# Both first experts freeze 384 slots in the last chunk of moe1, and expert 1's first layer is written ahead of expert 0's last slots

## The chip, the core and the metric

The kernel runs on one core of a Trainium2 chip. The metric is the device time of one execution in microseconds (us). Engines are named as the profile names them: PE is TensorE, ACT ScalarE, DVE VectorE, POOL GpSimd, and SP the engine that only issues transfers here.

## The reference, cut to what matters

Three stages follow each other: block-causal attention on 4 x 8 heads of 576 x 64, a dense gated layer on the 2304 tokens ("moe1"), and a mixture of eight experts with two experts for each token.

```
x   = attention(q, k, v)                  # 2304 x 512
x   = ((x @ w1) * (x @ w2)) @ w3 @ w_out  # moe1, inner width 1024
n   = x @ w_gate + log1p(exp(x @ w_noise)) * noise
top2, top2_w = the two largest of n, softmax over the two
for e in range(8):                        # the experts
    h = relu(x[tokens of e] @ m1[e])      # 512 -> 1024, "first layer"
    out[tokens of e] += top2_w * (h @ m2[e])   # 1024 -> 512, "second layer"
```

## The kernel before

Every product is made of three matmuls of float32r high and low parts (`mm3`, L470 to L472, on PE). What splits a matrix into the two parts is `split` (L457): a cast on ACT for the high part (L461) and a subtraction on DVE, or on POOL, for the low part (L465).

moe1 walks over nine chunks of 256 tokens. In a chunk, `ab` (L194) makes the gated product in eight steps f, and `yout` (L210) multiplies it with the folded product of w3 and w_out, which lies in the four weight buffers `pc[8]` to `pc[11]`. The router of a chunk (L249) runs one chunk later, in small pieces between these steps. At its end it scatters token numbers into a table in DRAM, `idt`, with four indirect transfers of 128 rows from POOL (L337), and SP writes the chunk's rows of y to DRAM, to `yt` (L356).

Each expert has 640 slots in the table, as five tiles of 128 ("slot tiles" 0 to 4). Slot tiles 0 to 2 are part s = 0, slot tiles 3 and 4 part s = 1. The work of an expert e on a part is: `gather` (L875), one indirect transfer from POOL for each slot tile, which reads 128 rows of y; `trans` (L884), four PE transposes a tile and a split into `xt`; `ffn1` (L896), the first layer, eight steps f of 12 matmuls, ended by a relu on ACT (L905) and a low part on DVE (L906); and `ffn2` (L908), the second layer, 24 matmuls a slot tile, ended by a scaling on ACT into the tile `yo` (L919) and an indirect transfer from POOL that adds the rows to the output (L920). `yo` has two buffers, and `xt` and `ht` of each part have one.

`freeze` (L419), called in the last chunk after all eight steps f, takes the router's count after eight chunks and makes sure that slots 0 to 383 of expert 0 are not written by the last chunk; it then calls `start_early` (L858), in which SP loads the table's rows of these slots (L864, tile `ids0`) and POOL gathers them (tile `xga`, three buffers). So expert 0's part 0 (`trans`, `ffn1`, `ffn2` at L503 to L506) runs while the last router ends. Everything else is in `phase3` (L922): SP loads the whole table (L926, tile `ids`) behind the last scatters, loads weights, and POOL gathers the other slots.

Weights of the experts come as 64 pieces of 0.5 MB, numbered n, eight for an expert (0 to 3 the first layer, 4 to 7 the second). `load_next` (L836) has SP load piece n into a staging tile and splits it into buffer `pc[ORDER[n % 12]]`. The first eight pieces are loaded early, in the last chunk, through the two staging tiles `xab` and `xr` (one buffer each); the others go through `stf` (three buffers) in `phase3`. Pieces 8 to 11, expert 1's first layer, go into `pc[8]` to `pc[11]`, which moe1 reads until its last `yout`.

A planner puts the instructions of each engine into one order from priorities and a model of durations, so the order on an engine isn't that of the code. Each engine then works strictly in its order.

Of the kernel before, what the change touches and what calls it, by code (L numbers as in the profile page):

```python
# [8 lines left out]
F32 = mybir.dt.float32  # L9
F32R = mybir.dt.float32r  # L10
BF16 = mybir.dt.bfloat16
I32 = mybir.dt.int32
I64 = mybir.dt.int64
AF = mybir.ActivationFunctionType
OP = mybir.AluOpType
# [7 lines left out]
P = 128  # L23
CAP = 640
NSLOT = CAP // P
NA = 3
# [55 lines left out]
class Moe1:  # L82
# [280 lines left out]
    def steps(self):  # L363

        state, due = {}, {}
        clock = [0]

        def ahead(c, last=3):

            step = state.get(c, 0)
            if c == NCH or step > last or clock[0] < due.get(c, 0) or (step == 0 and self.batches(c) > self.ready):
                return
            if step == 0:
                self.x_load(c)
            else:
                with ExitStack() as es:
                    for m in self.marks:
                        es.enter_context(self.tc.issue_after(m.ins))  # L380
                    self.x_prep(c, step - 1)
            state[c] = step + 1
            due[c] = clock[0] + (0 if c == 0 else AHEAD[step])

        for c in range(NCH):
            while state.get(c, 0) < 4:
                ahead(c)
                clock[0] += 2
                yield 0
            for f in range(8):  # L390
                while self.conv < 28 + 4 * (f // 2):
                    yield 0
                with self.tc.high_priority(offset=MOE_PRIO):
                    self.ab(c, f)
                self.tick(self.ticks)
                if c == NCH - 1 and f % 2 == 1:
                    self.k.load_next()
                    self.k.load_next()
                ahead(c + 1, 2)
                clock[0] += 1  # L400
                yield 2.67
            ahead(c + 1)
            if c == NCH - 1:
                for _ in self.rt:
                    pass
                self.freeze()
            for t in range(TPC):
                for part in range(2):
                    with self.tc.high_priority(offset=MOE_PRIO):
                        self.yout(c, t, part)  # L410
                    self.tick(self.ticks)
                    ahead(c + 1)
                    clock[0] += 1
                    yield 2.6
            for _ in self.rt:
                pass
            self.rt = self.router(c)

    def freeze(self):  # L419

        nc, p2, v = self.nc, self.p2, self.nc.vector
        cb = p2.tile([P, E], BF16, name="cb")
        v.tensor_copy(cb, self.run_cnt)
        pc = self.psR.tile([P, 512], F32, name="m")
        nc.tensor.matmul(pc[:, 0:1], self.tri[:, 1, :], cb[:, 0:1], start=True, stop=True)
        m = p2.tile([P, 1], F32, name="miss")
        v.tensor_tensor(m, self.room, pc[:, 0:1], op=OP.subtract)
        v.tensor_scalar(m, m, 0.0, float(NA), op0=OP.max, op1=OP.min)
        v.tensor_tensor(self.run_cnt[:, 0:1], self.run_cnt[:, 0:1], m, op=OP.add)
        self.k.start_early()  # L430

    def tail(self):
        nc, k, p2 = self.nc, self.k, self.p2
        self.ticks = 4
        self.psR = k.psT
        for _ in self.rest:
            pass
        for _ in self.rt:
            pass
        cb = p2.tile([P, E], BF16, name="cb")  # L440
        nc.vector.tensor_copy(cb, self.run_cnt)
        pcn = self.psR.tile([P, 512], F32, name="m")[:, 0:E]
        nc.tensor.matmul(pcn, self.tri[:, 1, :], cb, start=True, stop=True)
        cf = p2.tile([P, E + 1], F32, name="cf")
        nc.vector.tensor_copy(cf[:, 0:E], pcn)
        nc.vector.tensor_reduce(cf[:, E:], cf[:, 0:E], axis=AX, op=OP.max)
        nc.vector.tensor_copy(k.mxc, cf[:, E:])
        nc.vector.tensor_copy(k.cnt, cf[:, 0:E])


class Kernel:
# [23 lines left out]
    def run(self):  # L475
        tc, nc, a = self.tc, self.nc, self.a
        nc.scalar.preload_act_table_set("natural_log_exp_and_others")
        with ExitStack() as es:
            cp = es.enter_context(tc.tile_pool(name="cp", bufs=1))
            dr = es.enter_context(tc.tile_pool(name="dr", bufs=1, space=DRAM))  # L480
            self.cp = cp

            def dram(name, shape, dt=F32):
                return dr.tile(shape, dt, name=name)

            self.x2 = dram("x2", [BH, P, S])
            self.rs = dram("rs", [B, H, S])
            self.yt = dram("yt", [NT + P, ROW])
            self.idt = dram("idt", [E * TABR, 1], I32)
            self.ident = cp.tile([P, P], F32, name="ident")  # L490
            nc.sync.dma_start(self.ident, a["cst"][:, 0:128])
            self.pc = [cp.tile([P, 2, 1024], F32R, name=f"pc{i}") for i in range(12)]
            with ExitStack() as es2:
                self.psM = es2.enter_context(tc.tile_pool(name="psM", bufs=2, space=PSUM))
                with tc.tile_pool(name="p2", bufs=1) as self.p2:
                    self.moe1 = Moe1(self, self.p2, self.psM)
                    self.attention()
                    self.psT = es2.enter_context(tc.tile_pool(name="psT", bufs=2, space=PSUM, reuse_waits="tile"))
                    self.psH = es2.enter_context(tc.tile_pool(name="psH", bufs=4, space=PSUM, reuse_waits="tile"))
                    self.pa = es2.enter_context(tc.tile_pool(name="pa", bufs=1, side="right", reuse_waits="tile"))  # L500
                    self.early = True
                    self.moe1.tail()
                    self.trans(0, 0)  # L503
                    self.ffn1(0, 0)
                    for i in range(NA):
                        self.ffn2(0, i)  # L506
                    self.moe1.p2s.close()
                self.early = False
                self.phase3()
            self.overflow()  # L510
# [347 lines left out]
    def start_early(self):  # L858
        nc = self.nc
        self.xg, self.xt, self.ht, self.wv = {}, {}, {}, {}  # L860
        self.tab = self.idt.rearrange("(e s) o -> e (s o)", e=E)
        self.ids = self.pa.tile([P, E, NSLOT], I32, name="ids3")
        self.ids0 = self.pa.tile([P, NA], I32, name="ids0")
        nc.sync.dma_start(self.ids0, self.slots(self.tab, self.ids)[0][0][:, 0, :])  # L864
        self.gather(0, 0)

    def idx(self, e, i):
        ids = self.ids0[:, i:i + 1] if e == 0 and i < NA else self.ids[:, e, i:i + 1]
        return bass.IndirectOffsetOnAxis(ap=ids, axis=0)

    @staticmethod
# [3 lines left out]
    def gather(self, e, s):  # L875
        for i in self.part(s):
            if self.early:
                t = self.pa.tile([P, ROW], F32, name="xga", bufs=NA)
            else:
                t = self.pb.tile([P, ROW], F32, name="xg", bufs=8)  # L880
            self.xg[e, i] = t
            self.nc.gpsimd.indirect_dma_start(out=t, out_offset=None, in_=self.yt, in_offset=self.idx(e, i))
# [39 lines left out]
    def phase3(self):  # L922
        nc = self.nc
        with self.tc.tile_pool(name="pb", bufs=1, reuse_waits="tile") as self.pb:
            for src, dst in self.slots(self.tab, self.ids):
                nc.sync.dma_start(dst, src)  # L926
            for _ in range(4):
                self.load_next()
            self.gather(0, 1)
            self.gather(1, 0)  # L930
            self.gather(1, 1)
            for e in range(E):
                if e == 0:
                    self.trans(0, 1)
                else:
                    self.ffn1(e, 0)
                self.ffn1(e, 1)
                if e + 1 < E:
                    for s in range(2):
                        self.trans(e + 1, s)  # L940
                        if e + 2 < E:
                            self.gather(e + 2, s)
                for _ in range(4):
                    self.load_next()
                for i in range(0 if e else NA, NSLOT):
                    self.ffn2(e, i)
                for _ in range(4):
                    self.load_next()
# [96 lines left out]
```

## Time and profile before

| what | us |
|---|---|
| median of three runs | 1124.17 (1123.17 to 1125.45) |
| the profiled execution's own time | 1124.48 |
| its span, first to last instruction | 1122.7 |
| PE busy | 1056.7 (94%) |
| DVE, ACT, POOL busy | 575.1, 496.8, 367.5 |

All times in the text are counted from the start of the span of this one execution. moe1 ends at about 635 us, expert 0's part 0 at about 676 us, and the experts fill the rest. In the views of the trace a row names the line of the code, the engine, the operation and the tiles (output <- inputs). A bracket at a row's end tells how long the engine had stood idle before it and what ended that. The granted clock of TensorE is given as a share of full speed.

### The profile page before, as it was taken

Reading aid. Unit: us, or ns where it says so; the run is one execution under the profiler, and the core shown is the slowest. Engines: PE = TensorE matmul, PEld = TensorE weight load, DVE = VectorE, ACT = ScalarE, POOL = GpSimd, SP = SyncE. Lnnn points to the kernel's source line nnn. Section 1 sums busy time; section 2 is a strip of 40 time slices with the busy share of each in tenths; the row PEclk is TensorE's granted clock in tenths of the full one; section 3 lists DMA queues with packets and bytes.
Section 4 is the critical chain, followed back from the end, with each engine's and each line's share of the span. In section 5 each row is a group of like instructions: output and inputs, shape, how many; then the busy total and the mean of one; then the engine's idle time right before and its main releaser. Section 6 shows DMA issues by size and latency. Waiting matters only on the chain.

```text
span 1122.7 us, 17570 instructions
## 1 busy us (share of the span) xinstructions
PE 1056.7 (94%) x6588; PEld 945.3 (84%) x6588; DVE 575.1 (51%) x1229; ACT 496.8 (44%) x1180; POOL 367.5 (33%) x355
## 2 busy tenths in 40 slices
PE   5799978799999999999999898999999999999996
PEld 4577777698898989898999787989898989989894
DVE  6997779857475757653444434433334243424120
ACT  5765547565565647542234324433333333433120
POOL 4442445425243332523441326231312223120202
PEclk9998989998999999999999999999999999999998
DMA  9755775334615482524414227654444545351303
GB/s 231 247 185 164 197 174 193 95 93 119 165 63 117 142 207 76 116 70 81 77 38 95 86 81 224 187 141 104 133 112 123 122 123 122 104 113 30 38 10 40
DMA packets 79442, 135.81 MB, mean 121 GB/s; under 512 B 21005, under 2 KB 45813, under 8 KB 79349
## 3 DMA queue, kind: packets, MB, share of 16 engines
q1 hardware_dynamic: 69237, 113.44, 36.1%
q0 software_dynamic: 10112, 21.16, 10.2%
q8 instruction: 54, 0.88, 0.3%
q14 instruction: 39, 0.32, 0.1%
HBM read 103.92 MB, written 30.66 MB: 120 GB/s over the span
## 4 chain that ended last, share of the span: by engine, by line
PE 72%; DMA 10%; DVE 9%; issue 3%; ACT 2%; POOL 2%; SPq 2%; POOLq 0%; DVEq 0%; ACTq 0%
PE ph L470 12%; PE ph L472 12%; PE ph L471 12%; PE m L470 7%; PE m L471 7%; PE m L472 7%; PE tp L653 3%; PE av L678 3%; DMA stg<-in_w_dram 3%; DMA v<-in_v_dram 2%; PE sb L623 2%; PE sb L620 2%; DMA out_dram<-yo,ids 2%; DVE stf L529 2%; PE m L893 1%
## 5 line engine op out<-in xcount | busy, mean ns | idle before, releaser
L470 PE MATMUL m<-xh,pc 128*128 128x256 f32 x576 | 165.7, 291 | 2.0 <-DVE pc L465 0.8
L471 PE MATMUL m<-xh,pc 128*128 128x256 f32 x576 | 162.8, 287 | 3.1 <-DVE xh L465 3.1
L472 PE MATMUL m<-xh,pc 128*128 128x256 f32 x576 | 161.5, 287 | 0.3 <-POOL pc L465 0.3
L470 PE MATMUL ph<-xt,pc 128*128 128x256 f32 (+1 forms) x512 | 157.2, 309 | 4.8 <-issue 3.8
L471 PE MATMUL ph<-xt,pc 128*128 128x256 f32 (+1 forms) x512 | 157.8, 308 | 0.0
L472 PE MATMUL ph<-xt,pc 128*128 128x256 f32 (+1 forms) x512 | 157.5, 308 | 0.0
L920 POOL DMA_INDIRECT out_dram<-yo,ids x40 | 65.4, 1635 | 198.0 <-ACT yo L919 110.7
L906 DVE SCALAR_TENSOR_TENSOR ht<-ph,ht 128x256 fp32r<-128x256 f32 (+1 forms) x128 | 61.7, 489 | 130.3 <-ACT ht L905 129.7
L470 PE MATMUL ph<-pc,ht 128*128 128x512 f32 x320 | 128.0, 401 | 0.0
L471 PE MATMUL ph<-pc,ht 128*128 128x512 f32 x320 | 126.3, 395 | 0.0
L472 PE MATMUL ph<-pc,ht 128*128 128x512 f32 x320 | 126.2, 395 | 0.0
L461 ACT CAST pc<-stf 128x1024 fp32r<-128x1024 f32 (+1 forms) x96 | 82.1, 872 | 89.4 <-DMA stf<-in_m_dram 51.1
L465 DVE TENSOR_TENSOR pc<-stf,pc 128x1024 fp32r<-128x1024 f32 x56 | 67.4, 1226 | 104.7 <-ACT pc L461 97.6
L639 ACT ACTIVATE pb<-sb,nm 128x288 f32<-128x288 f32 (+3 forms) x192 | 93.6, 497 | 56.7 <-DVE nm L637 25.2
L470 PEld LDWEIGHTS m<-xh,pc 128*128 128x128 f32 x576 | 110.4, 193 | 4.2 <-DVE at L206 1.3
L471 PEld LDWEIGHTS m<-xh,pc 128*128 128x128 f32 x576 | 110.1, 193 | 4.3 <-DVE xh L465 3.7
L905 ACT ACTIVATE ht<-ph 128x256 fp32r<-128x256 f32 (+1 forms) x128 | 55.0, 437 | 127.6 <-PE ph L472 127.6
L472 PEld LDWEIGHTS m<-xh,pc 128*128 128x128 f32 x576 | 109.3, 193 | 1.2 <-POOL pc L465 0.8
L465 POOL TENSOR_TENSOR gt<-at,gt 128x256 fp32r<-128x256 f32 x72 | 57.8, 807 | 156.3 <-ACT gt L461 153.5
L653 PE MATMUL tp<-ident,pb 128*128 128x128 f32 x480 | 83.0, 289 | 23.3 <-ACT pb L639 8.4
L470 PEld LDWEIGHTS ph<-xt,pc 128*128 128x128 f32 x512 | 96.5, 189 | 5.6 <-issue 4.0
L634 DVE TENSOR_REDUCE nm<-sb 128x1 f32<-128x128 f32 (+2 forms) x192 | 79.2, 438 | 38.2 <-PE sb L623 32.9
(157 smaller groups left out, 2314.1 us busy)
## 6 DMA issues: line engine op xcount, KB each, us to landing
stf<-in_m_dram SPq DMA_DIRECT2D x56, 512.0 KB
qk<-in_qk_dram SPq DMA_DIRECT2D x32, 576.0 KB
stg<-in_w_dram SPq DMA_DIRECT2D x32, 512.0 KB
x<-ev SPq DMA_DIRECT2D x32, 288.0 KB
xab<-x SPq DMA_DIRECT2D x20, 256.0 KB
yt<-y SPq DMA_DIRECT2D x18, 260.0 KB
stg<-in_w_out_dram SPq DMA_DIRECT2D x8, 512.0 KB
v<-in_v_dram SPq DMA_DIRECT2D x24, 160.0 KB
```

The source lines that it names most:

```text
L461: d = nc.scalar.copy(h, src)
L465: return d, eng.tensor_tensor(l, src, r32(h), op=OP.subtract)
L470: nc.tensor.matmul(out, a, c, start=first, stop=False)
L471: nc.tensor.matmul(out, a, d, start=False, stop=False)
L472: nc.tensor.matmul(out, b, c, start=False, stop=last)
L634: nc.vector.tensor_reduce(nm[:, n:n + 1], o[:, 0:w], axis=AX, op=OP.max, negate=True)
L639: nc.scalar.activation(pb[t][:, k0:k0 + src.free_size()], src, AF.Exp, bias=nm, scale=1.0, accum_out=sums[:, h // H, t + n, h % H:h % H + 1])
L653: nc.tensor.transpose(bank[:, n * P:(n + 1) * P], pb[t][:, kt * P:(kt + 1) * P], self.ident)
L678: nc.tensor.matmul(c.av[:, o0:o0 + w], c.vv[:, kt, :], c.pt[:, i, s0:s0 + w], start=(kt == 0 and i == 0), stop=(kt == 4 and i == m - 1))
L905: nc.scalar.activation(hh[:, 0, f, :], ph, AF.Relu)
L906: nc.vector.scalar_tensor_tensor(hh[:, 1, f, :], ph, 0.0, r32(hh[:, 0, f, :]), op0=OP.max, op1=OP.subtract)
L920: nc.gpsimd.indirect_dma_start(out=self.a["out"], out_offset=self.idx(e, i), in_=yo, in_offset=None, compute_op=OP.add)
```

## The change

- `freeze` is called in the last chunk at step f = 5 and not after f = 7, and it freezes the 384 slots of expert 0 and of expert 1. `start_early` loads the table rows of both and gathers both (tile `xga` now has five buffers).
- The four pieces 8 to 11 are loaded in `tail`, through `xab` and `xr`, and no longer in `phase3` through `stf`.
- The whole table is loaded by POOL in two plain transfers (part 1's columns first), no longer by SP.
- Expert 0's part 1 is gathered early as well, and expert 1's `trans` and `ffn1` on part 0 are written ahead of `phase3`, that is, ahead of `trans` and `ffn1` of expert 0's part 1. `phase3` leaves out what has been done.

```diff
                 if c == NCH - 1 and f % 2 == 1:
                     self.k.load_next()
                     self.k.load_next()
+                if c == NCH - 1 and f == 5:
+                    for _ in self.rt:
+                        pass
+                    self.freeze()
...
             ahead(c + 1)
-            if c == NCH - 1:
-                for _ in self.rt:
-                    pass
-                self.freeze()
...
         for _ in self.rest:
             pass
+        for _ in range(4):
+            k.load_next()
         for _ in self.rt:
             pass
...
                     self.moe1.tail()
+                    for src, dst in reversed(self.slots(self.tab, self.ids)):
+                        nc.gpsimd.dma_start(dst, src)
+                    self.gather(0, 1)
                     self.trans(0, 0)
                     self.ffn1(0, 0)
                     for i in range(NA):
                         self.ffn2(0, i)
+                    self.trans(1, 0)
+                    self.ffn1(1, 0)
...
-        nc.sync.dma_start(self.ids0, self.slots(self.tab, self.ids)[0][0][:, 0, :])
+        nc.sync.dma_start(self.ids0, self.slots(self.tab, self.ids)[0][0][:, 0:2, :])
         self.gather(0, 0)
+        self.gather(1, 0)
...
-                t = self.pa.tile([P, ROW], F32, name="xga", bufs=NA)
+                t = self.pa.tile([P, ROW], F32, name="xga", bufs=NSLOT)
...
-            for src, dst in self.slots(self.tab, self.ids):
-                nc.sync.dma_start(dst, src)
-            for _ in range(4):
-                self.load_next()
-            self.gather(0, 1)
-            self.gather(1, 0)
             self.gather(1, 1)
             for e in range(E):
                 if e == 0:
                     self.trans(0, 1)
-                else:
+                elif e > 1:
                     self.ffn1(e, 0)
                 self.ffn1(e, 1)
                 if e + 1 < E:
                     for s in range(2):
-                        self.trans(e + 1, s)
+                        if e or s:
+                            self.trans(e + 1, s)
```

How the planner orders it is shown at three places. In these rows `pc_67` to `pc_78` are `pc[0]` to `pc[11]`, so `pc_75` to `pc_78` take the pieces 8 to 11; lines of the changed kernel are a few higher (`split` is at L463 and L467 there).

ACT at the end of moe1, from the last `gt` of moe1 to the high parts of expert 0's part 0 (`xt_7610` before, `xt_7638` in the change). Before:

```order
L222 COPY y<-m 128x512 x2
L461 CAST yT<-m 128x4x128
L461 CAST xt_7610<-m 128x4x128
L461 CAST yT<-m 128x4x128
L461 CAST xt_7610<-m 128x4x128 x2
```

In the change:

```order
L463 CAST pc_75<-xab 128x1024
L463 CAST pc_76<-xr 128x1024
L222 COPY y<-m 128x512 x2
L463 CAST pc_77<-xab 128x1024
L463 CAST yT<-m 128x4x128
L463 CAST xt_7638<-m 128x4x128
L463 CAST yT<-m 128x4x128
L463 CAST xt_7638<-m 128x4x128
L463 CAST pc_78<-xr 128x1024
L463 CAST xt_7638<-m 128x4x128
```

The four casts of the pieces now stand among the copies of y and the casts of yT and xt; DVE has the four low parts in the same places.

ACT after expert 0's first layer on part 0. Here `xt_7878` is expert 0's part 1 and `xt_8017` expert 1's part 0. Before:

```order
L461 CAST pc_75<-stf 128x1024
L919 ACTIVATE yo<-ph,wv_7611 128x512
L461 CAST pc_76<-stf 128x1024
L461 CAST pc_77<-stf 128x1024
L919 ACTIVATE yo<-ph,wv_7611 128x512
L461 CAST pc_78<-stf 128x1024
L461 CAST xt_7878<-m 128x4x128 x2
L461 CAST xt_8017<-m 128x4x128
L919 ACTIVATE yo<-ph,wv_7611 128x512
L905 ACTIVATE ht_7896<-ph 128x256 x7
```

In the change, where `xt_7869` is expert 1's part 0 and `xt_8025` expert 0's part 1:

```order
L463 CAST xt_7869<-m 128x4x128
L927 ACTIVATE yo<-ph,wv_7639 128x512 x3
L463 CAST xt_7869<-m 128x4x128 x2
L463 CAST xt_8025<-m 128x4x128 x2
L913 ACTIVATE ht_7895<-ph 128x384 x8
```

The casts of the pieces are gone from here, and all three `yo` now stand ahead of the last two casts of expert 1's part 0.

POOL, from the first gathers on. Before:

```order
L882 DMA xga<-yt,ids_7439 128x520 x3
L890 COPY wv_7611<-xga 128x1 x3
L337 DMA idt<-ids,si 18432x1 x4
L882 DMA xg<-yt,ids_7438 128x520 x8
L920 DMA out_dram<-yo,ids_7439 2432x512
```

In the change:

```order
L890 DMA xga<-yt,ids_7369 128x520 x5
L898 COPY wv_7639<-xga 128x1 x3
L890 DMA xga<-yt,ids_7369 128x520
L898 COPY wv_7870<-xga 128x1 x3
L337 DMA idt<-ids,si 18432x1 x4
L506 DMA ids_7368<-idt 128x8x2
L506 DMA ids_7368<-idt 128x8x3
L890 DMA xga<-yt,ids_7368 128x520 x2
L890 DMA xg<-yt,ids_7368 128x520 x2
L928 DMA out_dram<-yo,ids_7369 2432x512
L890 DMA xg<-yt,ids_7368 128x520 x6
```

The two table loads now stand on POOL behind the last scatters, and four gathers, not eight, stand ahead of the first addition to the output.

## Rows read from the trace of the kernel before

**Rows 1.** The page: PE's busy time, share of the span, instructions.

```profile
PE 1056.7 (94%) x6588; PEld 945.3 (84%) x6588; DVE 575.1 (51%) x1229; ACT 496.8 (44%) x1180; POOL 367.5 (33%) x355
```

**Rows 2.** Busy time by stretch: length, PE, PEld, DVE, ACT, POOL, then granted clock.

```profile
760.00:1100.00 340.00, 340.00 (x1956) 307.59 (x1955) 109.58 (x161) 113.88 (x190) 71.35 (x70) 1.00 0.40 94
```

**Rows 3.** PE in order of time, behind expert 0's part 0: start, length.

```profile
676.41 1.03 PE L893 MATMUL m<-ident,xg 128*128 128x128 f32 x8
681.19 0.62 PE L470 MATMUL ph<-xt,pc 128*128 128x256 f32 x3 [3.75 <-issue]
...
689.37 0.39 PE L470 MATMUL ph<-xt,pc 128*128 128x256 f32 x1 [1.05 <-ACT yo L919]
```

**Rows 4.** The same columns as rows 2, around the fall of the clock.

```profile
682.00:682.50 0.50, 0.35 (x3) 0.36 (x4) 0.50 (x2) 0.00 (x0) 0.50 (x5) 1.00 0.99 398
682.50:683.00 0.50, 0.50 (x4) 0.32 (x3) 0.19 (x1) 0.00 (x0) 0.03 (x1) 0.53 1.06 416
...
685.50:686.00 0.50, 0.50 (x4) 0.50 (x4) 0.00 (x0) 0.00 (x0) 0.50 (x1) 0.56 1.13 225
```

**Rows 5.** The chain that ended last, 655 to 700: start, length, what.

```profile
659.80 4.86 DMA idt<-ids,si
...
665.13 3.72 DMA ids<-idt
...
668.92 0.74 issue
669.67 5.07 DMA xg<-yt,ids
...
680.23 8.29 DMA out_dram<-yo,ids
...
688.63 0.70 ACT yo L919
...
690.35 0.12 PE ph L470
...
696.71 0.87 PE m L893 x8
```

**Rows 6.** POOL in order of time.

```profile
672.23 0.95 POOL L882 DMA_INDIRECT xg<-yt,ids  x1 [0.30 <-issue]
...
689.32 1.62 POOL L920 DMA_INDIRECT out_dram<-yo,ids  x1 [1.81 <-ACT yo L919]
...
694.56 1.59 POOL L920 DMA_INDIRECT out_dram<-yo,ids  x1 [3.19 <-DMA out_dram<-yo,ids]
```

**Rows 7.** ACT in order of time, the same stretch.

```profile
679.12 1.04 ACT L461 CAST pc<-stf 128x1024 fp32r<-128x1024 f32 x1 [3.42 <-DMA stf<-in_m_dram]
680.07 1.07 ACT L461 CAST xt<-m 128x512 fp32r<-128x512 f32 x2
```

**Rows 8.** SP's queue at the end of moe1.

```profile
664.68 1.02 SPq L926 DMA_DIRECT2D ids<-idt  x2
```

**Rows 9.** DVE, ACT and PE at the end of moe1, each from its own timeline.

```profile
623.47 1.23 DVE L465 TENSOR_TENSOR pc<-xab,pc 128x1024 fp32r<-128x1024 f32 x1 [0.99 <-ACT pc L461]
...
636.31 0.59 ACT L461 CAST yT<-m 128x512 fp32r<-128x512 f32 x1 [0.26 <-PE m L229]
...
640.35 0.63 PE L893 MATMUL m<-ident,xga 128*128 128x128 f32 x4 [0.87 <-DMA xga<-yt,ids]
```

**Rows 10.** The chain again, 600 to 622: loads of weight pieces.

```profile
605.05 5.56 DMA xr<-in_m_dram
...
613.02 4.57 DMA xr<-in_m_dram
```

**Rows 11.** PE in order of time, behind a short idle in attention.

```profile
180.36 0.55 PE L653 MATMUL tp<-ident,pb 128*128 128x128 f32 x3 [2.10 <-DVE ev L668]
```

**Rows 12.** The same columns as rows 2, behind that idle.

```profile
182.00:184.00 2.00, 2.00 (x11) 1.96 (x11) 1.40 (x3) 1.54 (x4) 1.42 (x2) 0.50 0.62 176
```

**Rows 13.** ACT in order of time, behind expert 0's last slots.

```profile
714.37 1.05 ACT L461 CAST pc<-stf 128x1024 fp32r<-128x1024 f32 x1 [2.42 <-DMA stf<-in_m_dram]
```

More of the change, by code (lines that the diff above doesn't have):

```diff
@@ L424, in freeze @@
         pc = self.psR.tile([P, 512], F32, name="m")
-        nc.tensor.matmul(pc[:, 0:1], self.tri[:, 1, :], cb[:, 0:1], start=True, stop=True)
-        m = p2.tile([P, 1], F32, name="miss")
-        v.tensor_tensor(m, self.room, pc[:, 0:1], op=OP.subtract)
+        nc.tensor.matmul(pc[:, 0:2], self.tri[:, 1, :], cb[:, 0:2], start=True, stop=True)
+        m = p2.tile([P, 2], F32, name="miss")
+        v.tensor_tensor(m, self.room.broadcast_to([P, 2]), pc[:, 0:2], op=OP.subtract)
         v.tensor_scalar(m, m, 0.0, float(NA), op0=OP.max, op1=OP.min)
-        v.tensor_tensor(self.run_cnt[:, 0:1], self.run_cnt[:, 0:1], m, op=OP.add)
+        v.tensor_tensor(self.run_cnt[:, 0:2], self.run_cnt[:, 0:2], m, op=OP.add)
         self.k.start_early()
@@ L862, in start_early @@
         self.ids = self.pa.tile([P, E, NSLOT], I32, name="ids3")
-        self.ids0 = self.pa.tile([P, NA], I32, name="ids0")
-        nc.sync.dma_start(self.ids0, self.slots(self.tab, self.ids)[0][0][:, 0, :])
+        self.ids0 = self.pa.tile([P, 2, NA], I32, name="ids0")
+        nc.sync.dma_start(self.ids0, self.slots(self.tab, self.ids)[0][0][:, 0:2, :])
         self.gather(0, 0)
+        self.gather(1, 0)
     def idx(self, e, i):
-        ids = self.ids0[:, i:i + 1] if e == 0 and i < NA else self.ids[:, e, i:i + 1]
+        ids = self.ids0[:, e, i:i + 1] if e < 2 and i < NA else self.ids[:, e, i:i + 1]
         return bass.IndirectOffsetOnAxis(ap=ids, axis=0)
```

## Prediction

> **What bounds the kernel now.** I read the page first, then the busy time by stretches, then PE, ACT and POOL in order of time and the chain of waits around the seam between moe1 and the experts. PE is busy for 94% of the span [rows 1], and from 760 to 1100 it has no idle time at all [rows 2]. So what PE gains before 690 us lasts to the end, and work on other engines counts only where PE waits for it. The seam is such a place. Behind expert 0's part 0 PE does eight transposes, idles 3.75 us, works, and idles 1.05 us more [rows 3]. The clock is granted in full until 682.5, at half (1.2 GHz) until about 685.7, and then in full again [rows 4], which costs half of 3.2 us, 1.6. In all, from 676.41 to 696.71 [rows 3, 5] there are 20.3 us for 12 transposes of 0.11 (0.87 for eight) and 96 matmuls of 0.12 [rows 5], 1.3 + 11.5 us. **The seam loses 7.5 us.** The first idle ends when ACT casts xt, and ACT is late because the cast of a weight piece waits for its load until 679.12 [rows 7]. The second hangs on a longer chain: last scatter, table load, eight gathers, the first addition to the output, and the third `yo`, which needs that addition's buffer and starts at 688.63 [rows 5].
>
> **The change part by part.** *The freeze at step 5* moves nothing: PE's matmul that counts the slots stands at the same place of its order, and the load of `ids0` still waits for the scatters of chunk 7. Counting two experts instead of one is two columns instead of one, at no cost that a row of DVE or PE could show.
>
> *Pieces 8 to 11 come early.* Their loads and casts leave the seam, and with them the cause of the 3.75 us. They now stand between moe1's last steps and expert 0's first layer. The first takes `xab` when DVE has done with piece 6, at 623.47 + 1.23 = 624.7 [rows 9]. It lands 4.6 to 5.6 us later [rows 10], its cast (1.04 [rows 7]) and low part (1.23) end near 632.3, and only then can piece 10 be loaded. It lands near 637.3 (5.0, between the two rows) and its cast ends at 638.4. ACT's order puts the casts of yT and xt behind it, and the first ran at 636.31 before [rows 9]: 2.1 us late. Part of that is hidden, since PE waited there for the gathers anyway (0.87 [rows 9] and two such waits), and the DVE low parts then run back to back. I put expert 0's first layer 1.0 us later, 0.5 of it for four transposes that are only moved: **0.5 us lost**, between 0 and 2.1. The router's last chunk gets about 0.5 us later with it.
>
> *What stands in the seam now.* PE's order is: expert 0's second layer (ends at 676.4 + 1.0 = 677.4), 16 transposes (1.8 us, till 679.2), expert 1's first layer. That layer needs the casts of xt, and ACT has all three `yo` ahead of the last two of these. The third `yo` needs the first addition to have landed. So **a chain that cost 1.05 us before now stands squarely in PE's way**:
> - The last scatter lands at 659.80 + 4.86 = 664.7 [rows 5]; I take 665.7, 0.5 for the later router and an estimated 0.5 because SP no longer holds its weight loads behind the table load at 664.68 [rows 8], so that they run beside the scatters.
> - POOL issues the table's load. No row of before has a plain transfer from POOL. Below, it is SP's 0.5 each [rows 8]; above, 1024 short runs at the 0.95 of a POOL transfer of 128 rows [rows 6] make 7.6 each. POOL's own transfers take 0.95 to 1.62 whatever their rows hold [rows 6], so I take 1.5. The gathers need only the first load. It lands 3.3 us after its issue (3.72 from the second's start, less 0.4 of issue [rows 5, 8]), and 0.74 us pass until the first gather [rows 5]: 671.2, against 669.67 before.
> - Four gathers at 1.25 (0.95 and 0.30 of idle [rows 6]) instead of eight: the addition is issued at 676.2.
> - It lands 5.2 us later in one row (689.32 to 694.56 [rows 6]) and 8.29 in another, with eight gathers and weight loads ahead of it [rows 5]. I take 5.9, near the first, since half of the gathers and all of those loads are gone: 682.1.
> - The third `yo` 0.70 [rows 5], two casts 1.1 [rows 7]: PE goes on at 684.0.
>
> PE idles 684.0 - 679.2 = 4.8 us and loses 1.6 to the clock as before, and with the 0.5 from above that is 6.9 against 7.5. **The sum is a gain of 0.6 us.** From the profiled execution's 1124.48 that is 1123.9; this execution lies 0.3 above the median of the runs, so by the median it is 1123.6. What is late next after the cast is the addition's landing, and nothing behind 690 us covers a loss.
>
> The row shows SP's table load landing 3.72 us after its last issue [rows 5]. The Trainium skill (DMA: Bandwidth & Descriptors, "Issuing engine by pattern" and "Specifications") speaks against this part of the change: simple loads belong on Sync, and the first byte of a GpSimd transfer takes about 1 us against about 0.6. As an estimate by that page the first gather would come 0.4 us later than with the load on SP, and the sum would be a gain of about 0.8; no row of before shows it.
>
> *The rest.* The `ids0` load doubles to 256 short runs, and three more gathers of 1.25 us stand on POOL at 637 to 641, where POOL has nothing else to do until the scatters. Later pieces, gathers and transposes of `phase3` only keep their places, except as in the last rival.
>
> **The rivals.**
> - *Faster: the short end of the chain.* Table loads at 0.5 and an addition in 5.2 give 1.0 + 0.7 more, a gain of 2.3 us, 1121.9. Should the clock hold through the remaining 3.1 us of idle, 1.6 more, 1120.3. Against the last speaks that an idle of 2.10 us was followed by half clock in attention [rows 11, 12].
> - *Slower: POOL's table loads.* They decide from 2.1 us each, where the gain is gone. From 3.4 us on the gathers wait for POOL itself, which has to issue both loads, and each further microsecond counts twice. At 5.0 each the first gather starts at 676.3, 5.1 later than above: 4.5 lost, 1128.7. For it speaks the count of runs, against it the flat price of POOL's rows. The upper bound of 7.6 would give 1133.9.
> - *Slower: piece 10 holds ACT up.* Its load shares the engines with five gathers. If it lands 2.5 us later, yT and the whole chain move as much, and PE idles over 2 us near 640, which the clock may answer as in rows 12 for 1.6 us: 1127 or so. It decides from 0.6 us.
> - *Slower: the relus of expert 1's part 1.* ACT has them behind the cast of the eighth piece loaded after expert 0's last slots; in before that cast ends at 715.4 [rows 13], 18.7 us behind 696.7. The layer that followed then had 384 columns, and its fifth step came late enough. Now it has 256. Eight transposes (0.9), two slot tiles (48 matmuls of 512 columns, 11.2) and four steps of 1.4 bring PE to the fifth step after 17.7 us, where it needs the first relu's buffer, free at 19.5. That is 1.8 idle and 1.6 of clock, 2.8 lost in the sum, 1127.0. Against it: three of these pieces are now loaded ahead, so the row may be too late.
> - *It doesn't do what it says.* The order shows expert 1's layer ahead, so only the freeze is an empty step, and that is in the sum.
>
> **How the numbers follow.** A measurement of this kernel can tell 0.2%, some 2.2 us, from no change. The forecast (within that bound, its own range 1121.9 to 1126.4) has 0.42, the faster case 0.22, the three slower ones 0.13, 0.10 and 0.13, together 0.36. The range goes from 1120.0, the short chain with the clock held, to 1130.0, which takes in the three slower cases and leaves out the dear end of the table loads and sums of two of them.
>
> **What would show it.** In the changed kernel's trace: the load of piece 10 ends ACT's wait before yT, at 637 to 638, and expert 0's first layer starts about 1 us later; two table loads on POOL of 1 to 2 us each, the first gather behind them near 671; the first addition lands near 682, and ACT's third `yo` ends its wait on it; PE idles near 5 us between the transposes and expert 1's first layer, with half clock behind it; no idle time after that. The forecast is wrong if PE doesn't wait for the third `yo` (then it is faster by up to 4 us), if a table load on POOL takes over 3 us, if PE waits over 2 us at 636 to 644, or if it waits for a relu between 711 and 745.

## The result, and the profile after

| kernel | median us (lowest to highest, runs) | profiled execution: time, span, mean granted clock |
|---|---|---|
| before | 1124.81 (1123.17 to 1128.54, 6) | 1124.48, 1122.7, 0.979 |
| changed | 1131.84 (1129.50 to 1137.60, 6) | 1131.66, 1129.8, 0.974 |

The changed kernel takes 1.0056 times as long, with an interval of 1.0033 to 1.0079. It is slower by about 7 us (1131.84 - 1124.81 = 7.03), where "no change" was forecast, and it lies above the range.

PE's instructions are as many as before (6588) and the experts still run without a gap from 760 to 1100; this row of the changed kernel has the columns of [rows 2]:

```profile
760.00:1100.00 340.00, 340.00 (x1956) 307.56 (x1955) 109.66 (x161) 113.91 (x190) 73.67 (x72) 1.00 0.39 94
```

So the time was lost at the seams. PE of the changed kernel in order of time (start, length, line, operation; in brackets the idle time before it and what ended it):

```profile
641.05 1.11 PE L901 MATMUL m<-ident,xga 128*128 128x128 f32 x4 [6.62 <-DMA xga<-yt,ids]
...
688.71 1.65 PE L472 MATMUL ph<-xt,pc 128*128 128x384 f32 x4 [5.01 <-issue]
...
738.91 0.38 PE L472 MATMUL ph<-xt,pc 128*128 128x256 f32 x1 [1.31 <-DVE ht L914]
```

The second row is the seam on which the prediction rests: 5.01 us, in place of 3.75 and 1.05 [rows 3]. The third is a small new wait. **The first is where most of the time went**: 6.62 us of idle ahead of expert 0's first transposes, where PE before waited three times for under 1 us each (the last of them in [rows 9], 0.87).

The clock fell there too. Stretches of the changed kernel with the columns of [rows 2], those at the first seam and then those at the second:

```profile
636.00:640.00 4.00, 0.00 (x0) 0.00 (x0) 1.46 (x2) 1.53 (x2) 3.08 (x4) 0.60 0.86 279
640.00:644.00 4.00, 2.95 (x13) 2.73 (x14) 1.38 (x3) 1.27 (x3) 2.90 (x6) 0.50 0.73 212
644.00:648.00 4.00, 4.00 (x21) 3.75 (x20) 2.88 (x4) 2.29 (x4) 0.71 (x4) 0.62 0.24 68
...
688.00:692.00 4.00, 3.29 (x10) 3.29 (x11) 2.48 (x4) 1.64 (x4) 3.22 (x8) 0.50 0.78 208
692.00:696.00 4.00, 4.00 (x17) 4.00 (x17) 0.56 (x1) 0.49 (x1) 1.89 (x4) 0.64 0.73 128
```

In the kernel before, the same stretch of the first seam is granted in full:

```profile
636.00:640.00 4.00, 2.14 (x16) 1.47 (x14) 1.98 (x3) 2.30 (x5) 1.42 (x4) 1.00 0.63 178
640.00:644.00 4.00, 3.65 (x24) 3.26 (x25) 1.57 (x3) 1.14 (x3) 0.18 (x1) 1.00 0.00 0
```

What PE waits for at 641 is told by the chain of waits of the changed kernel (start, length, what):

```profile
623.93 7.73 DMA idt<-ids,si
...
631.67 3.16 DMA ids<-idt
...
635.82 5.18 DMA xga<-yt,ids
```

The same links in the kernel before:

```profile
625.83 5.42 DMA idt<-ids,si
...
631.27 1.60 DMA ids<-idt
```

In the kernel before, the chain goes on with the last of three gathers. The first, which is the one to compare, is issued at 633.85, and PE takes up its rows at 637.19 (the first row is POOL, the second PE):

```profile
633.85 0.98 POOL L882 DMA_INDIRECT xga<-yt,ids  x1 [4.27 <-DMA ids<-idt]
637.19 0.66 PE L893 MATMUL m<-ident,xga 128*128 128x128 f32 x4 [0.92 <-DMA xga<-yt,ids]
```

Chunk 7's last scatter takes 2.3 us longer, the load of `ids0` 1.6 longer (it also has twice the rows), and the first gather lands in 5.18 us, where it was 3.3. Beside each of them the changed kernel has a load of a weight piece. SP's queue in the changed kernel:

```profile
622.82 0.33 SPq L859 DMA_DIRECT2D xab<-in_m_dram  x1
626.13 0.33 SPq L859 DMA_DIRECT2D xr<-in_m_dram  x1
...
633.23 0.33 SPq L859 DMA_DIRECT2D xab<-in_m_dram  x1
634.51 0.33 SPq L859 DMA_DIRECT2D xr<-in_m_dram  x1
```

Pieces 8 and 9 stand beside the scatters, pieces 10 and 11 beside the first gathers. In the kernel before, SP issues nothing from 622.95 to 631.27.

**One execution against another.** The stage with attention doesn't take the same time in each execution (the runs of one kernel here lie up to 12 us apart, and in the nine traces its last matmuls start between 491 and 501 us), and it is over before the seams. So beside the medians I use a second measure from each profiled execution: the time from the start of chunk 7's last scatter, as the chain of waits has it, to the end of the span. Before it is 1122.7 - 625.83 = 496.9 us, in the changed kernel 1129.8 - 623.93 = 505.9: 9.0 us more. It is one execution each; the medians remain the verdict.

By place: at the first seam 6.62 of idle against 0.92 + 0.42 + 0.87 = 2.21, +4.4; PE's busy time there at a lower clock, 2.95 x 0.50 + 4.00 x 0.38 = +3.0. At the second, 5.01 against 3.75 + 0.33 + 1.05 = 5.13, -0.1; the clock, 3.29 x 0.50 + 4.00 x 0.36 = 3.1 against 1.6, +1.5; the new wait, +1.3. The sum is 10.1, close to the 9.0. The first seam is 7.4 of it.

### The profile page after: what moved, and what is told of

The parts are those of the page before. It is cut to its first block, busy times and chain, and to the rows that moved or that the text cites. A ratio compares the mean times of both kernels' runs of the same rounds, so it can differ in the third digit from the quotient of the medians.

```text
span 1129.8 us, 17563 instructions
## 1 busy us (share of the span) xinstructions
PE 1060.9 (94%) x6588; PEld 949.7 (84%) x6588; DVE 576.1 (51%) x1229; ACT 496.1 (44%) x1180; POOL 366.6 (32%) x357
## 4 chain that ended last, share of the span: by engine, by line
PE 73%; DVE 11%; DMA 8%; issue 4%; ACT 2%; POOL 1%; SPq 0%; POOLq 0%; DVEq 0%; ACTq 0%
PE ph L472 12%; PE ph L473 12%; PE ph L474 12%; PE m L472 8%; PE m L473 8%; PE m L474 8%; PE tp L660 3%; PE av L685 3%; PE sb L630 2%; PE sb L627 2%; DVE stf L536 2%; DVE stf L537 2%; DMA stg<-in_w_dram 1%; PE m L901 1%; DVE stf L535 1%
## 5 line engine op out<-in xcount | busy, mean ns | idle before, releaser
L472 PE MATMUL ph<-xt,pc 128*128 128x384 f32 (+1 forms) x512 | 157.6, 310 | 6.3 <-issue 5.0
L473 PE MATMUL ph<-xt,pc 128*128 128x384 f32 (+1 forms) x512 | 158.1, 309 | 0.0
L474 PE MATMUL ph<-xt,pc 128*128 128x384 f32 (+1 forms) x512 | 157.9, 308 | 0.0
L914 DVE SCALAR_TENSOR_TENSOR ht<-ph,ht 128x384 fp32r<-128x384 f32 (+1 forms) x128 | 61.8, 489 | 134.1 <-ACT ht L913 132.6
L913 ACT ACTIVATE ht<-ph 128x384 fp32r<-128x384 f32 (+1 forms) x128 | 55.2, 437 | 135.8 <-PE ph L474 131.5
L467 DVE TENSOR_TENSOR pc<-stf,pc 128x1024 fp32r<-128x1024 f32 x52 | 62.6, 1225 | 93.9 <-ACT pc L463 87.0
L463 ACT CAST pc<-stf 128x1024 fp32r<-128x1024 f32 (+1 forms) x92 | 78.0, 864 | 71.4 <-DMA stf<-in_m_dram 35.6
L467 POOL TENSOR_TENSOR gt<-at,gt 128x256 fp32r<-128x256 f32 x72 | 57.5, 803 | 155.3 <-ACT gt L463 152.5
```

Source lines behind the costliest of these rows:

```text
L463: d = nc.scalar.copy(h, src)
L467: return d, eng.tensor_tensor(l, src, r32(h), op=OP.subtract)
L472: nc.tensor.matmul(out, a, c, start=first, stop=False)
L473: nc.tensor.matmul(out, a, d, start=False, stop=False)
L474: nc.tensor.matmul(out, b, c, start=False, stop=last)
L913: nc.scalar.activation(hh[:, 0, f, :], ph, AF.Relu)
```

## The experiments

Two theories stood at the start. **Collision**: the four weight loads of 0.5 MB each, moved into moe1's end, share the DMA engines with the small transfers on which expert 0's start hangs. **More rows**: it is the second expert's tables and the three further gathers that hold up the first. Times are against the runs of the kernel before that stood beside them: their median is 1125.31 for the early loads, the tables, the held loads and the third tile in the changed kernel, and 1124.53 for the other three. A ratio is estimated from all runs, so it isn't quite the quotient of two medians.

### The early loads alone

The kernel before, with the four loads in moe1's tail as in the change, and out of `phase3`:

```
+        for _ in range(4):
+            k.load_next()
...
-            for _ in range(4):
-                self.load_next()
```

> The kernel before with one part of the change alone: pieces 8 to 11 are loaded in tail through xab and xr, and no longer in phase3. Freeze, table loads, gathers and the order of the layers stay as before. Theory A (the early weight loads collide with the last scatters of chunk 7, the load of ids0 and the first gathers): the last of these scatters lands over 7 us after its issue (5.42 in the kernel before, 7.73 in the changed one), and PE waits over 4 us for the first gather behind moe1 (0.92 before, 6.62 changed). Theory B (the doubled ids0 and the two or three more gathers do it): scatter near 5.4, PE's wait near 1 us. The time: A 1129 to 1134, B 1122 to 1126.

Measured: 1131.40, ratio 1.0068 (1.0041 to 1.0094). From the last scatter to the end: 1130.0 - 624.09 = 505.9, as much as the whole change. Its chain and its PE:

```profile
624.09 8.55 DMA idt<-ids,si
...
632.66 2.15 DMA ids<-idt
...
635.79 5.57 DMA xga<-yt,ids
```

```profile
641.40 1.12 PE L895 MATMUL m<-ident,xga 128*128 128x128 f32 x4 [6.00 <-DMA xga<-yt,ids]
```

PE waits 6.00 us there, and 1.30 for the copy of y just before (0.44 in the kernel before). PE's clock falls as in the changed kernel: 2.60 us of work from 640 to 644 at 0.50 and 4.00 from 644 to 648 at 0.69. By the same sum as above the first seam loses 6.00 + 1.30 - 2.21 - 0.44 = 4.7 of idle and 2.5 of clock, 7.2 in all, where the changed kernel lost 7.4. **The early loads, out of all parts of the change, make the whole loss of the first seam.**

That the totals agree too (505.9) is in part chance, since the rest of them is made of other things. In the changed kernel it is the clock at the second seam and the wait at 738.91. Here PE waits longer at the second seam, 8.42 us where it was 5.13:

```profile
684.03 4.91 DMA out_dram<-yo,ids
689.04 0.69 ACT yo L921
```

```profile
690.74 1.22 PE L472 MATMUL ph<-xt,pc 128*128 128x256 f32 x4 [8.42 <-ACT xt L463]
```

With the casts of the pieces gone from this seam, the third `yo` and the first addition, still behind eight gathers, stand in PE's way in the old order of layers as well.

### Both tables and gathers alone

```
-        self.ids0 = self.pa.tile([P, NA], I32, name="ids0")
-        nc.sync.dma_start(self.ids0, self.slots(self.tab, self.ids)[0][0][:, 0, :])
+        self.ids0 = self.pa.tile([P, 2, NA], I32, name="ids0")
+        nc.sync.dma_start(self.ids0, self.slots(self.tab, self.ids)[0][0][:, 0:2, :])
         self.gather(0, 0)
+        self.gather(1, 0)
```

(with the freeze of both experts behind step 8, where it was, and `gather(1, 0)` dropped from `phase3`)

> The kernel before with the other part alone: both experts freeze, ids0 holds the rows of both, and expert 1's first three slot tiles are gathered early (xga has five buffers); pieces 8 to 11 stay in phase3. Theory A (weight loads collide): the last scatter of chunk 7 lands in about 5.4 us, PE's wait for the first gather stays under 2 us, the time is within 2 us of the kernel before. Theory B (twice the rows and more gathers): PE waits over 4 us for the first gather and the time is 4 us or more above the kernel before.

Measured: 1124.95, ratio 1.0003 (0.9981 to 1.0025); from the last scatter to the end 1122.9 - 625.60 = 497.3. "More rows" falls. Its links are near those of before, and PE waits once for 2.56 us instead of three times for 2.21 together. That is over the 2 us that were expected, and the clock falls behind it (0.80 from 636 to 640, 0.77 from 640 to 644), but the time is the same:

```profile
625.60 6.10 DMA idt<-ids,si
...
631.72 1.82 DMA ids<-idt
```

### Two of the four loads early

The kernel before, with pieces 8 and 9 loaded in moe1's tail and 10 and 11 left in `phase3`:

```
+        for _ in range(2):
+            k.load_next()
...
-            for _ in range(4):
+            for _ in range(2):
                 self.load_next()
```

> The kernel before with pieces 8 and 9 loaded at moe1's last chunk, as in the change, and pieces 10 and 11 left where they were, behind the whole early part. With all four early the time rose 7.7 us and PE waited 6.0 us for the first early gather. Collision theory: 8 and 9 lie beside the last scatters and make these land late (8.6 us against 5.4), 10 and 11 lie beside the gathers (5.6 us against 3.3); so two bring about half to two thirds: PE waits 3.5 to 4.5 us, time 1127 to 1130. Rival one: a queue or buffer wait that pieces 10 and 11 alone make (their buffers come free late): no loss, 1124 to 1126. Rival two: any early piece costs all of it: 1131 to 1133.

Measured: 1126.81, ratio 1.0014 (0.9996 to 1.0033); from the last scatter to the end 1121.9 - 621.33 = 500.6, +3.7 of the 9.0. PE's wait of 4.31 us is as expected, and the time lies just under its range. By the runs alone a loss is not certain. The links separate the loads:

```profile
621.33 8.37 DMA idt<-ids,si
...
629.72 2.68 DMA ids<-idt
...
633.38 3.34 DMA xga<-yt,ids
```

```profile
636.77 0.85 PE L895 MATMUL m<-ident,xga 128*128 128x128 f32 x4 [4.31 <-DMA xga<-yt,ids]
```

With 8 and 9 early, scatter and table load are as late as with all four; with 10 and 11 gone from there, the gather is at 3.34 instead of 5.57. So each link is lengthened by the loads that run beside it.

### The loads held behind the gathers

The changed kernel, with its four loads behind expert 0's early gathers (a one-column memset on POOL, which has to come after the last of them, stands ahead of pieces 8 and 9), and their casts behind expert 0's first layer:

```
-        for _ in range(4):
-            k.load_next()
...
                     self.ffn1(0, 0)
+                    for _ in range(4):
+                        self.load_late()
```

> The changed kernel, but the loads of pieces 8 and 9 wait until POOL has issued the early gathers, and the casts of the pieces 8 to 11 stand behind the last relu of expert 0's first layer on part 0; pieces 10 and 11 are loaded when those have freed the staging tiles. Theory A: the last scatter of chunk 7 lands in about 5.4 us, ids0 in about 3, PE's wait for the first gather falls from 6.62 to 1 to 2 us, no half clock at 637 to 647, and the time falls by 5 to 8 us from the changed kernel's 1131.8, to 1124 to 1127. Theory B: the wait stays over 4 us, the time within 2 us of the changed kernel's. By both, the 5 us of idle before expert 1's first layer stay, since the third yo still waits for the first addition.

Measured: 1126.98, ratio to before 1.0017 (1.0001 to 1.0033); from the last scatter to the end 1125.7 - 624.26 = 501.4, 4.5 less than the changed kernel. The links are those of "both tables" again, and so is PE's wait. The time is in the expected range, but two things were not as expected: the wait is 2.53 us and not 1 to 2, and the clock fell after all (0.50 from 636 to 640, 0.65 from 640 to 644).

```profile
624.26 6.24 DMA idt<-ids,si
...
630.51 1.83 DMA ids<-idt
...
633.33 3.29 DMA xga<-yt,ids
```

```profile
636.66 1.11 PE L917 MATMUL m<-ident,xga 128*128 128x128 f32 x4 [2.53 <-DMA xga<-yt,ids]
...
685.38 1.65 PE L470 MATMUL ph<-xt,pc 128*128 128x384 f32 x4 [3.97 <-ACT xt L461]
```

The second row is the second seam, which this edit leaves.

### A third output tile

The changed kernel with three `yo` tiles (32 bytes per partition for it come from two small router tiles made one):

```
-        yo = self.pa.tile([P, DM], F32, name="yo", bufs=2)
+        yo = self.pa.tile([P, DM], F32, name="yo", bufs=3)
```

> The changed kernel with three buffers for yo (and one tile of the router shared to make room). Theory: the 5.01 us of PE idle ahead of expert 1's first layer hang on the third yo, which waits for the first addition's buffer, and ACT holds the casts of xt behind it. Then that idle time falls under 1.5 us, the clock stays full there, and the time falls by 5 to 7 us, to 1125 to 1127. Rival: the layer waits for the gather of expert 0's part 1 or for the pieces; then the idle time stays over 3 us and the time within 2 us of the changed kernel's. The 6.6 us behind moe1 stay by both.

Measured: 1124.51, ratio to before 0.9992 (0.9976 to 1.0009), 7.3 us under the changed kernel; from the last scatter to the end 1120.3 - 623.82 = 496.5, 9.4 less. The time is half a microsecond under the expected range. At the second seam PE doesn't wait at all and the clock stays, from 688 to 692 too; with the columns of [rows 2]:

```profile
684.00:688.00 4.00, 4.00 (x25) 4.00 (x24) 0.64 (x2) 0.49 (x1) 3.06 (x4) 1.00 0.84 232
```

The first seam is nearly as bad as in the changed kernel (1.12 and 5.40 us of idle), so the two losses are separate. This shows that the addition's landing, through the third `yo`, is what the 5.01 us wait for: nothing else on that path was edited.

### The third tile in the kernel before

> The kernel before with three yo tiles instead of two, and nothing else. If the third tile's gain belongs to the change (in the kernel before, the wait of 3.75 us at the seam is for a gather, and only the 1.05 us behind it is for a yo tile), this takes 0.5 to 1.5 us off before: 1123.5 to 1124.8. Rival: the addition is what both kernels wait for, directly or through POOL's queue, and the tile brings before as much as the change: 4 to 7 us, 1118 to 1121; the early order would then have no part in it.

The same two lines of diff on the kernel before. Measured: 1126.42, ratio 0.9994 (0.9975 to 1.0013); from the last scatter to the end 1126.4 - 629.37 = 497.0. It brings nothing, not even the 1.05 us; the median lies outside both ranges that were given, but the interval holds "no change". PE waits 5.58 us for a cast of xt, and ACT has that behind a weight piece:

```profile
683.48 1.04 ACT L461 CAST pc<-stf 128x1024 fp32r<-128x1024 f32 x1 [4.31 <-DMA stf<-in_m_dram]
...
685.01 1.06 ACT L461 CAST xt<-m 128x512 fp32r<-128x512 f32 x2
```

In the old order the weight piece sets the end and the tile hides behind it; once the pieces are loaded early, as in the change, the tile sets the end (the early loads alone showed it, with 8.42 us). The gain belongs to the change and the tile together.

### Both: loads held, and the third tile

> The changed kernel with two edits together: the loads of pieces 8 and 9 held behind expert 0's early gathers (10 and 11 follow them, their casts behind expert 0's first layer), and three yo tiles. Collision theory: the two losses lie at different places, so the gains add. Alone the late pieces took 4.9 us off the changed kernel (1131.84 to 1126.98) and the third tile 7.3 us (to 1124.51); together 12.2, 1119.6, and at least 3 us under before: 1118.5 to 1122. PE idle 2.5 us ahead of the first early transposes, under 2 us between expert 0's last early slot and its first late product. Rival: the two are not independent, since with late pieces PE also waited for gathers of expert 1 between the addition's wait and the slot before (0.78 and 0.82 idle), and a POOL queue that has the held memsets and the gathers to do stays the bound: 1123 to 1125.

Measured: 1123.15, ratio to before 0.9972 (0.9951 to 0.9992), 8.7 us under the changed kernel and **the one version that is faster than the kernel before**. From the last scatter to the end it takes 1124.2 - 631.21 = 493.0, 3.9 less than before and 12.9 less than the changed kernel; alone the two edits gave 4.5 and 9.4. By that stretch the gains add nearly in full, but part of it is the first seam of this one execution: there PE waits in three pieces (0.85, 0.34 and 0.71 us) with the clock in full, where with the loads held alone it waited 2.53 us at once and lost the clock, though both have the same edits at that place. Why they differ is open. By the medians less is left than expected: the time lies in the rival's range of 1123 to 1125 and 1.4 us under before, where 3 were asked for (by the ratio it is 3.1). The rival's waits are there too:

```profile
643.16 0.66 PE L917 MATMUL m<-ident,xga 128*128 128x128 f32 x4 [0.85 <-DMA xga<-yt,ids]
...
646.08 0.63 PE L917 MATMUL m<-ident,xga 128*128 128x128 f32 x4 [0.71 <-DMA xga<-yt,ids]
...
684.20 0.63 PE L917 MATMUL m<-ident,xga 128*128 128x128 f32 x4 [0.67 <-DMA xga<-yt,ids]
...
733.38 0.39 PE L470 MATMUL ph<-xt,pc 128*128 128x256 f32 x1 [1.30 <-DVE ht L930]
```

None of them is over 1.3 us, and the granted clock is 1.00 in every stretch from 610 to 1100. The waits at 684 to 686 (0.67 and 0.79 us) may have the old cause in a new place: POOL's two table loads, at 672.43, now have weight loads beside them (SP issues five from 668.60 to 672.34), and the first gather starts at 680.63, 8.2 us later, where it took 676.77 - 672.27 = 4.5 in the changed kernel. No run tried this by itself.

## Why the prediction was wrong, point by point

**The step that failed: "Pieces 8 to 11 come early", put at 0.5 us lost and bounded at 2.1.** It followed the loads to their own users (buffer, landing, cast, ACT's order), and that part held: piece 10's cast was put at an end of 638.4 and runs from 637.46 to 638.50. But PE didn't wait for it: it stood until 641.05 for the gather. The step took the scatters, the load of `ids0` and the gathers at their old durations, though it put two megabytes of loads on the engines that carry them. What it measured: +4.4 us of idle and +3.0 of clock, 7.4 in place of 0.5; with the early loads alone the same seam lost 7.2. The upper bound of 2.1 was wrong in kind: it bounded ACT's delay only. The rival "piece 10 holds ACT up" named the cause in half a sentence ("its load shares the engines with five gathers") and then priced the wrong victim: piece 10's own load came as forecast, and the scatter, the table load and the gathers came late.

**What stands in the seam.** The chain was the right one, and the idle came out as 5.01 for 4.8, with luck. The seam came late: PE was ready at 683.70 for 679.2, and the last scatter started at 664.71, where 660.3 was put; being late alike, these leave the idle as it is. Then two errors of a like size cancel. The last scatter landed 7.27 us after its start, where 4.86 and an estimated 0.5 stood, 1.9 more: the same collision, with phase 3's `stf` loads, which SP no longer holds behind the table load. The other traces bear it out: this scatter took 4.80 to 5.00 us in the five kernels in which SP holds these loads, and 6.22, 6.28 and 7.27 in three of those in which it doesn't. From that landing to PE's going on it took 688.71 - 671.98 = 16.7 us, where 684.0 - 665.7 = 18.3 was put, 1.6 less. The changed kernel's chain there:

```profile
664.71 7.27 DMA idt<-ids,si
...
672.27 1.86 DMA ids<-idt
...
681.92 4.99 DMA out_dram<-yo,ids
...
687.01 0.70 ACT yo L927
```

- POOL's table loads: 1.86 us both together, 0.93 each, where the prediction took 1.5 each (bounds 0.5 and 7.6). That rival is out.
- The first gather, 4.8 us after the scatters' landing (676.77 - 671.98), where the prediction took 5.5; with the load on SP it was 5.0, 669.67 - 664.66 [rows 5].
- Four gathers ahead of the addition, 681.92 - 676.77 = 5.15, where the prediction took 5.0; the addition's landing 4.99 for 5.9.
- The clock: 3.1 us lost instead of 1.6. The half-granted stretch lasted some 3.2 us before [rows 4] and from 688 to about 694.8 here. PE was busy nearly all through both, and why one was twice as long is open.

The 0.4 us against GpSimd that the prediction estimated from the Trainium skill (DMA: Bandwidth & Descriptors, "Specifications") is not to be seen in 4.8 against 5.0, though other transfers differ between the two kernels as well.

**The relus of expert 1's part 1**: 1.31 us of idle at 738.91, and it is there in each kernel with the new order (0.96 to 1.31), so the rival came true in part. It was put at 1.8, and the clock, which the prediction let fall, stayed full. ACT and DVE of the changed kernel show what makes it: both stand for a piece's load, and DVE makes the piece's low part ahead of that of the relus, for which PE waits:

```profile
736.22 1.05 ACT L463 CAST pc<-stf 128x1024 fp32r<-128x1024 f32 x1 [2.04 <-DMA stf<-in_m_dram]
737.30 1.23 DVE L467 TENSOR_TENSOR pc<-stf,pc 128x1024 fp32r<-128x1024 f32 x1 [2.44 <-ACT pc L463]
738.44 1.41 DVE L914 SCALAR_TENSOR_TENSOR ht<-ph,ht 128x256 fp32r<-128x256 f32 x4
```

It was given as an alternative to the forecast, with 0.13; it was rather a term to add.

**The freeze and the second expert's tables**: no cost put, none measured in the time (ratio 1.0003). The call at step 5 itself was not tried alone.

**The signs to look for** were right: "if PE waits over 2 us at 636 to 644" was among what would make the forecast wrong, and it is what happened. The other times from 660 on came some 4.5 to 5.6 us later than put (the first addition landed at 686.91 for 682.1).

**What stays open.** The version with both edits is ahead of the kernel before by 0.8 to 4.9 parts in a thousand; how much of its remaining waits could go was not tried, nor was the table load put back on SP in the new order. And where the small transfers meet the loads, on the DMA engines or in the memory behind them, no run separates.

## What to carry to other kernels

A load that is moved into a quiet stretch of the DMA queues is not free because its own user can wait: list the small transfers that run there on the critical chain and price them as lengthened. Where a change puts a chain squarely on the path, look at which buffer count closes it; the tile that was worth nothing in the old order was worth 7 us in the new one. And price a wait of PE together with the clock behind it, since in the changed kernel waits of 5.01 and 6.62 us cost some 3 more each in half clock.

## What the runs showed of the hardware

**Bulk loads lengthen a small scatter by half.** The landing of chunk 7's last scatter took 5.42 and 5.19 us in two kernels with no load beside it, 5.74 to 6.24 in three with the second expert's tables (why it is longer there is open: they are loaded only after it), and 7.73 to 8.55 in four with weight loads. The last chunk's scatter says the same, with 4.80 to 5.00 against 6.22 to 7.27. Transfers by queue (packets, MB, share of the 16 engines' time) show what changes. POOL's queue is q0; in these stretches it has only the scatters. In the changed kernel from 624 to 628, and then from 628 to 632:

```profile
q1 hardware_dynamic: 60, 0.21, 72.0%
q0 software_dynamic: 4, 0.00, 2.8%
```

```profile
q1 hardware_dynamic: 236, 0.84, 55.7%
q0 software_dynamic: 64, 0.00, 1.1%
```

In the kernel before, q0 from 626 to 628, and then the stretch from 628 to 632 with the columns of [rows 2] and, behind the clock, the engines' busy share and GB/s:

```profile
q0 software_dynamic: 68, 0.00, 2.5%
```

```profile
628.00:632.00 4.00, 3.80 (x17) 2.94 (x17) 0.32 (x1) 0.41 (x1) 1.32 (x2) 1.00 0.00 0
```

Before, the scatters' packets are through by 628, and the landing at 631.25 comes over 3 us later, with nothing on the engines. In the changed kernel 64 of them pass only after 628, though scatters take only 1 to 3% of the engines' time: they pass late, while SP's transfers keep the engines busy. From 624 to 628 these take 72% of the engines' time and move only 0.21 MB, a quarter of what they move in the next four microseconds; what slows them there no run here shows.

The Trainium skill (DMA: Bandwidth & Descriptors, "Queues, rings and completion order") says that an engine serves its queues in turn, a whole packet at a time. The longer landings agree with that; how much of them it explains, no run here shows.

**The clock after idle time.** PE waits of 2.53 to 6.62 us at the first seam were followed by stretches granted below 1.00 in all six kernels that had them; in the three that waited for 0.30 to 1.13 us at a time, the clock stayed full.
